# Values in rows of 1 KB beside one block of ones, S2 through GpSimd's queue, three more sums by DMA and a new order: sketched attention followed by a rational mixture layer

## The chip, the cores and the metric

One Trainium2 chip, one of its cores. The metric is the device time of one execution in microseconds (us). Three runs of the kernel before gave 252.32, 252.56 and 252.72, so its median is 252.56 us.

## What is computed

The attention replaces the softmax by a product of two linear sketches of 8 columns each, so keys and queries become 64 features per head. A rational function stands between two matrix products behind it.

```python
def phi(x):                                   # 32 -> 64 features
    a = np.einsum('rd,bhsd->bhsr', S1, x)
    b = np.einsum('rd,bhsd->bhsr', S2, x)
    return np.einsum('bhsi,bhsj->bhsij', a, b).reshape(*x.shape[:-1], 64)
q_p, k_p = phi(q), phi(k)                     # batch 4, heads 4, 1088 tokens
kv = np.einsum('bhsf,bhsd->bhfd', k_p, v)
z = np.sum(k_p, axis=2)
x = einsum(q_p, kv) / (einsum(q_p, z) + 1e-6) # -> [4352, 128]
h = x @ w_in                                  # [4352, 2048]
P = a[0] + a[1]*h + a[2]*h**2 + a[3]*h**3
Q = 1 + |b[0]|*|h| + |b[1]|*h**2
out = (P / (Q + 1e-6)) @ w_out                # [4352, 128]
```

## The kernel before

**Tiles and groups.** The 4352 tokens are cut into chunks of 512. The first chunk is split into two of 256 (called 0 and 0b), and the last, also of 256, holds the 64 tokens of each batch that don't fill a chunk. For each chunk the hidden layer (2048 columns, 16 blocks of 128) is worked in groups. Groups 0 to 3 are the blocks of chunk 0 (2, 2, 4 and 8 of them), group 4 is the whole of chunk 0b, groups 5 to 18 are two for each of the seven full chunks, and groups 19 to 22 (8, 4, 3 and 1 blocks) belong to the last chunk. A full group is a tile of 128x4096.

**One group.** TensorE multiplies `h` into PSUM (L793, a tile of 128x1024 at a time). ScalarE copies it to bf16 as `hb` (L799). For the groups in CASTS one of these four copies is made by VectorE. VectorE takes |h| into `u` (L808, step abs) and h squared into `lin` (L816, step sq). The sum `u += lin` (step +Q) gives the denominator, from which ScalarE makes 1/Q with a logarithm (L830, step Ln, which writes `L`) and an exponential (L833, step Exp, back into `u`). VectorE builds the numerator in `y` (L820 odd, L826 oddt, L823 even), then `y += lin` (step +P), then y times u (step n5, L826), and TensorE multiplies by w_out (L846). The letters in PLANS say who does what in a group: with Q or P that sum is done by a DMA which adds in flight (L882, issued by GpSimd), without it by VectorE (L878). With z the constant term of the numerator is given to TensorE as a second product with a scaled w_out (`w_out_0`), and VectorE's step even is left out. A new letter, s, which is already in the code, lets ScalarE make the square.

**Attention.** Keys of a batch are transposed (L451), copied (L455), sketched (L460), copied (`ab`, L467) and multiplied into features (`k_p`, L478), then summed against the values (L495, kv). The values stand in `v_aug`, head by head, 32 columns and a column of ones beside each, so a matmul takes 66 columns for two heads and the column of ones gives z. For batch 0 the values land in a spare tile first and GpSimd copies them (L437); for the other batches four DMAs write them in pieces of 128 bytes. Queries go a like way (L601, L611, L649, L657), and x comes from L669. Chunks 0 and 0b come early: they don't wait for the matrix W_abc, but take numerator and denominator from one product (L677), add 1e-6 (L688), invert (L692) and divide (L698).

**What sets the order.** Every step is put into a plan with its predecessors. The table ORDER, 773 step numbers, says in what order the steps are issued, and each engine works through its own steps in that order. A step that waits holds back everything behind it on its engine. DMAs of one issuer are likewise started in order. Buffers are counted in BUFS: three each of hb, u, lin and y. SyncE's queue (SP) holds the loads and stores, ScalarE's queue S1 and S2, and GpSimd's queue (POOL) the small loads and the sums by DMA. The steps called hot (L1002) are products of zeros that keep TensorE occupied.

Of the kernel before, what the change touches and what calls it, by code (L numbers as in the profile page):

```python
# [123 lines left out]
def kernel(  # L124
# [74 lines left out]
    v_aug = [big.tile([128, H, J, D + 1], FP, name=f"v_aug{i}") for i in range(2)]  # L199

    def load_main(eng, name, src, b, part=None):
        src = src[b, :, 0:MAIN, :].rearrange("h (p j) d -> p h j d", j=J)
        if name == "v_sb" and b > 0:
            for h in range(H):
                QUEUE[eng].dma_start(out=v_aug[b % 2][:, h, :, 0:D], in_=src[:, h])
            return
# [214 lines left out]
    def scale_w(dst, scale, half):  # L421
        hs = slice(half * NF // 2, (half + 1) * NF // 2)
        if dst is w_out_b:
            return lambda: nc.vector.tensor_scalar(out=dst[:, hs, :], in0=w_out_f[:, hs, :], scalar1=scale, scalar2=None, op0=AX.mult)
# [613 lines left out]
```

## Time and profile before

| | before |
|---|---|
| time, median of 3 runs | 252.56 us (252.32 to 252.72) |
| profiled execution, its own time | 252.38 us |
| span of that execution | 250.7 us |
| granted TensorE clock | 1.00 |
| DMA traffic | 38.51 MB, of it 27.27 MB by GpSimd's queue |
| packets under 512 bytes | 17968 of 31807 |

The profile shows one execution. The span runs from the first to the last instruction; 1.68 us of the execution's own time lie around it. "Busy" is the time in which an engine has at least one instruction under way. Since an instruction is often begun before its predecessor has left the pipe, durations of neighbours overlap, and what an instruction really takes from its engine is the distance between two starts. In a timeline row the first number is the start, the second the duration, and the bracket at the end tells how long the engine stood idle before and what ended that.

### The profile page before, as it was taken

How to read it: one execution, taken by the hardware profiler on the slowest of the kernel's cores; microseconds unless marked ns; L12 is line 12 of the kernel's file. 1: busy time of each engine (PE TensorE's matmuls, PEld its weight loads, DVE VectorE, ACT ScalarE, POOL GpSimd, SP SyncE). 2: the span in 40 equal slices, each digit the busy share in tenths (PEclk: the TensorE clock that was granted, in tenths of full speed). 3: DMA queues.
4: the chain of work that ended last, by engine and by line, in shares of the span. 5: the costliest groups of instructions: out<-in, count | busy, mean ns of one | idle time of the engine just before them, and what ended most of it. 6: DMA issues, size and time to landing. Idle time of an engine off the chain costs nothing.

```text
span 250.7 us, 3050 instructions
## 1 busy us (share of the span) xinstructions
PE 239.3 (95%) x1124; PEld 142.6 (57%) x1135; DVE 229.0 (91%) x243; ACT 221.9 (89%) x201; POOL 49.9 (20%) x68
## 2 busy tenths in 40 slices
PE   8989999999999999999999999999999999999873
PEld 4878888655559655665554544444435444664541
DVE  0647999799999999999999999999999999999991
ACT  3435594799999999999999999999999999999992
POOL 5728003010301113001051101132111111130100
PEclk9999999999999999999999999999999999999999
DMA  6997581998548649980849999598999999699622
GB/s 159 290 280 148 135 150 29 153 221 186 92 76 152 120 86 180 188 156 15 155 84 192 203 190 171 103 181 157 188 181 186 184 168 185 114 223 188 126 86 64
DMA packets 31807, 38.51 MB, mean 154 GB/s; under 512 B 17968, under 2 KB 23600, under 8 KB 31664
## 3 DMA queue, kind: packets, MB, share of 16 engines
q0 software_dynamic: 7152, 27.27, 61.7%
q1 hardware_dynamic: 24208, 10.95, 17.5%
q8 instruction: 9, 0.15, 0.2%
q10 hardware_dynamic: 432, 0.10, 0.2%
q14 instruction: 6, 0.05, 0.1%
HBM read 8.82 MB, written 2.23 MB: 44 GB/s over the span
## 4 chain that ended last, share of the span: by engine, by line
ACT 52%; PE 18%; DVE 12%; issue 10%; DMA 6%; SPq 1%; ACTq 0%
ACT L L830 17%; ACT u L833 16%; ACT hb L799 11%; PE h_ps L793 8%; DVE y L826 4%; DMA u<-lin 4%; PE w_ps L495 3%; DVE y L820 2%; ACT q_pT L663 2%; DMA k_rem<-in_k_dram 2%; ACT o_sb L851 2%; PE w_ps L657 1%; PE w_ps L460 1%; PE w_ps L1002 1%; ACT xT L717 1%
## 5 line engine op out<-in xcount | busy, mean ns | idle before, releaser
L793 PE MATMUL h_ps<-xT,w_in_sb 128*128 128x512 f32 (+1 forms) x320 | 125.6, 532 | 0.7 <-ACT hb L799 0.6
L793 PEld LDWEIGHTS h_ps<-xT,w_in_sb 128*128 128x128 f32 x320 | 58.2, 190 | 43.0 <-issue 34.1
L799 ACT CAST hb<-h_ps 128x1024 bf16<-128x1024 f32 (+2 forms) x65 | 70.4, 1124 | 6.5 <-PE h_ps L793 6.4
L830 ACT ACTIVATE L<-u,one_ap,kappa 128x4096 f32<-128x4096 bf16 (+5 forms) x23 | 70.5, 3066 | 0.0
L833 ACT ACTIVATE u<-L 128x4096 bf16<-128x4096 f32 (+5 forms) x23 | 66.2, 2879 | 0.1
L882 POOL DMA_DIRECT2D u<-lin x16 | 22.2, 1391 | 129.8 <-ACT u L833 31.2
L816 DVE TENSOR_TENSOR lin<-hb 128x4096 bf16<-128x4096 bf16 (+5 forms) x23 | 39.7, 1727 | 2.5 <-ACT hb L799 2.3
L826 DVE TENSOR_TENSOR y<-y,u 128x4096 bf16<-128x4096 bf16 (+5 forms) x23 | 39.7, 1727 | 0.6 <-ACT u L833 0.3
L826 DVE TENSOR_TENSOR y<-y,hb 128x4096 bf16<-128x4096 bf16 (+5 forms) x23 | 39.7, 1726 | 0.0
L846 PE MATMUL out_ps<-y,w_out_b 128*128 128x512 bf16 (+1 forms) x139 | 30.3, 354 | 1.7 <-DVE y L826 1.5
L820 DVE TENSOR_SCALAR y<-lin,a_t 128x4096 bf16<-128x4096 bf16 (+5 forms) x23 | 24.4, 1059 | 0.0
L846 PEld LDWEIGHTS <-w_out_b 128*128 128x128 bf16 x144 | 14.0, 98 | 16.8 <-issue 5.7
L882 POOL DMA_DIRECT2D y<-lin x11 | 14.2, 1287 | 44.7 <-DVE lin L823 20.8
L808 DVE TENSOR_SCALAR u<-hb 128x4096 int16<-128x4096 int16 (+5 forms) x23 | 21.7, 945 | 0.0
L878 DVE TENSOR_TENSOR y<-y,lin 128x4096 bf16<-128x4096 bf16 (+5 forms) x12 | 15.7, 1306 | 0.1
L495 PE MATMUL w_ps<-v_aug,k_p 128*128 128x66 f32 x128 | 15.7, 272 | 0.0
L495 PEld LDWEIGHTS w_ps<-v_aug,k_p 128*128 128x128 f32 x128 | 15.0, 192 | 1.0 <-issue 0.8
L823 DVE TENSOR_SCALAR lin<-lin,a_t 128x4096 bf16<-128x4096 bf16 (+5 forms) x16 | 14.0, 877 | 1.6 <-DMA u<-lin 1.6
L663 ACT COPY q_pT<-w_ps 128x512 f32<-128x512 f32 (+1 forms) x20 | 12.4, 631 | 3.3 <-PE w_ps L657 3.3
L846 PE MATMUL out_ps<-u,w_out 128*128 128x512 bf16 x55 | 13.0, 379 | 0.0
L478 DVE TENSOR_TENSOR k_p<-ab 128x1024 f32<-128x1024 f32 x8 | 9.8, 1219 | 2.6 <-ACT ab L467 2.6
L1002 PE MATMUL w_ps<-const-float32-0.0 128*128 128x512 bf16 x45 | 11.8, 380 | 0.3
(110 smaller groups left out, 224.1 us busy)
## 6 DMA issues: line engine op xcount, KB each, us to landing
u<-lin POOLq DMA_DIRECT2D x15, 1024.0 KB, 8.7
y<-lin POOLq DMA_DIRECT2D x10, 1024.0 KB, 9.7
out_dram<-oT SPq DMA_DIRECT2D x7, 256.0 KB, 2.6
kq<-in_k_dram SPq DMA_DIRECT2D x3, 512.0 KB, 6.4
v_aug<-in_v_dram SPq DMA_DIRECT2D x12, 128.0 KB, 4.8
kq<-in_q_dram SPq DMA_DIRECT2D x3, 512.0 KB, 4.8
w_in_sb<-in_moe_w_in_dram SPq DMA_DIRECT2D x1, 1024.0 KB, 6.9
kq<-in_k_dram SPq DMA_DIRECT2D x2, 256.0 KB, 3.1
```

Of the source, the lines that this page charges most:

```text
L495: nc.tensor.matmul(T["kv", b][:, hp * 66:(hp + 1) * 66], lhsT=lhs(hp), rhs=rhs(hp), start=(first and hp == 0), stop=final, skip_group_chec ...
L663: nc.scalar.copy(out=T["q_pT", n][:, hp, :W], in_=T["qpTp", n, hp][:, :W])
L793: nc.tensor.matmul(T["h", g, s][:, i * W:(i + 1) * W], lhsT=w_in_sb[:, fi * 128:(fi + 1) * 128], rhs=T["xT", n][:, :W], start=True, stop=True)
L799: copy(out=T["t", g][:, s * W:(s + nsub) * W], in_=T["h", g, s][:, :nsub * W])
L808: nc.vector.tensor_scalar(out=u().bitcast(mybir.dt.int16), in0=ht().bitcast(mybir.dt.int16), scalar1=0x7FFF, scalar2=None, op0=AX.bitwise_and)
L816: nc.vector.tensor_mul(out=sq(), in0=ht(), in1=ht())
L820: nc.vector.tensor_scalar(out=y(), in0=sq(), scalar1=a_t[:, 3:4], scalar2=a_t[:, 1:2], op0=AX.mult, op1=AX.add)
L826: return lambda: nc.vector.tensor_mul(out=out(), in0=in0(), in1=in1())
L830: nc.scalar.activation(out=T["L", g][:, :gw], in_=u(), func=ACT.Ln, bias=one_ap, scale=kappa[:, 2:3])
L833: nc.scalar.activation(out=u(), in_=T["L", g][:, :gw], func=ACT.Exp, scale=-1.0)
L846: nc.tensor.matmul(T["o", n][:, :W], lhsT=w[:, fi, :], rhs=T[src, g][:, i * W:(i + 1) * W], start=(start and i == 0), stop=(stop and i == ...
L882: nc.gpsimd.dma_start(out=dst(), in_=src(), accum_op=AX.add, max_dma_last_dim=GW)
```

## The change

The values stand in `v_aug` as [128, 5, 8, 32]: blocks 1 and 3 hold heads 0 and 1, blocks 0 and 4 heads 2 and 3, and block 2 is all ones and shared by the two pairs. The DMA now writes rows of 1 KB, two DMAs for a batch, and for batch 0 straight into place, so that GpSimd's two copies go. A matmul takes 96 columns for a pair. The values of the leftover tokens are laid out in a like way.

S1 stays on ScalarE's queue, S2 goes to GpSimd's as its first instruction. The identity has a step of its own, and the transposes wait for that alone. `ab` has two buffers instead of one. In chunks 0 and 0b the 1e-6 is put in by a small product with the identity (`den_eps`) before numerator and denominator are added, so VectorE's addition L688 goes. The scaled w_out is made by ScalarE instead of VectorE. The bias of the logarithm is a number in the instruction instead of a tile. XWARM falls from two products of zeros to none.

Groups 8, 11 and 14 get their sum +P by DMA. Group 12 loses z, and group 4 gets s. Groups 11, 13 and 15 give one more copy of h to VectorE. The groups of chunk 0 and those of the last chunk each share one buffer of every kind (PACKED), in place of one buffer per group. ORDER is new throughout; of it the first row is shown.

```diff
-    0, 4, 50, 54, 2, 6, 51, 5, 8, 10, 1, 3, 52, 12, 69, 7, 9, 14, 74, 70, 55, 16, 11, 71, 53, 75, 67, 18, 13, 96,
+    0, 4, 5, 56, 2, 7, 9, 51, 6, 11, 1, 52, 53, 3, 69, 13, 8, 54, 10, 15, 74, 70, 57, 17, 12, 71, 58, 75, 55, 59,
...
-    PLANS = {**{g: "QP" for g in range(4, 20)}, **{g:"Q" for g in (5,8,11)},**{g:"Qz" for g in (14,17)},**{g:"QPz" for g in (12,13,15,16,18)}}
-    CASTS = {18:(6,),16:(6,),14:(6,),12:(6,),17:(6,)}
-    XWARM = (2, 0)
+    PLANS = {**{g: "QP" for g in range(4, 20)}, 5:"Q",17:"Qz",**{g:"QPz" for g in (13,15,16,18)},4:"sQP",14:"QPz"}
+    CASTS = {18:(6,),16:(6,),14:(6,),12:(6,),17:(6,),13:(6,),15:(6,),11:(6,)}
+    PACKED = (0, 9)
+    XWARM = (0, 0)
...
-                kq=3, v_aug=2, kT=2, ab=1, k_p=2, qT=1, abc=1, q_p=1, q_pT=2, den=1,
+                kq=3, v_aug=2, kT=2, ab=2, k_p=2, qT=1, abc=1, q_p=1, q_pT=2, den=1,
...
-    v_aug = [big.tile([128, H, J, D + 1], FP, name=f"v_aug{i}") for i in range(2)]
+    PAIRS = (slice(1, 4, 2), slice(0, 5, 4))
+    WITH_ONES = (slice(1, 4), slice(0, 5, 2))
+    v_aug = [big.tile([128, 2 * NP + 1, J, D], FP, name=f"v_aug{i}") for i in range(2)]
...
         if name == "v_sb":
-            if part == 0:
-                T[name, b] = tile_of(att, "q_p", [128, JC * H, R * R], FP).rearrange("p (h a) (c d) -> p h (a c) d", h=H, d=D)
-            hs = slice(2 * part, 2 * part + 2)
-            QUEUE[eng].dma_start(out=T[name, b][:, hs], in_=src[:, hs])
+            for hp in range(NP) if part is None else (part,):
+                QUEUE[eng].dma_start(out=v_aug[b % 2][:, PAIRS[hp]], in_=src[:, 2 * hp:2 * hp + 2])
             return
...
-    last_of["ACT"] = plan.add("ACT", 1300, lambda: load_small("ACT"), rank=-99, name="load")
+    last_of["ACT"] = plan.add("ACT", 650, lambda: load_small("ACT", 0), rank=-99, name="load")
+    i = plan.add("POOL", 1500, lambda: load_small("POOL", 1), rank=-99.9, name="load S2")
...
-            return lambda: nc.vector.tensor_scalar(out=dst[:, hs, :], in0=w_out_f[:, hs, :], scalar1=scale, scalar2=None, op0=AX.mult)
+            return lambda: nc.scalar.activation(out=dst[:, hs, :], in_=w_out_f[:, hs, :], func=ACT.Copy, scale=scale)
...
-        for hps in pairs:
-            kb.append(plan.add("DVE", 200 if b else 270, lambda hps=hps: kv_blocks(hps), after=[sums[-1], c_ms] + kb[-1:],
+        for hps, done in zip(pairs, sums):
+            kb.append(plan.add("DVE", 200 if b else 270, lambda hps=hps: kv_blocks(hps), after=[done, c_ms] + kb[-1:],
...
+        def den_eps(t):
+            T["nd", n, t] = tile_of(aps, "w_ps", [128, CW], FP)
+            nc.tensor.matmul(nd_parts(t)[0][:, :, 2 * D:], lhsT=ident,
+                             rhs=den_t[n % BUFS["den"]][:, 0:8, R].rearrange("p (g h) -> p g h", h=2), start=True, stop=False,
+                             skip_group_check=True)
...
-            nc.scalar.activation(out=T["L", g][:, :gw], in_=u(), func=ACT.Ln, bias=one_ap, scale=kappa[:, 2:3])
+            nc.scalar.activation(out=T["L", g][:, :gw], in_=u(), func=ACT.Ln, bias=1.0 + 1e-6, scale=kappa[:, 2:3])
```

Three places of the new order matter below. The first is TensorE at the start, where the keys of batch 0 are sketched and summed against the values (S is the sketch, kT the transposed keys, k_p their features). Before:

```order
L460 MATMUL w_ps<-S_105,kT 128x64 x4
L601 MATMUL w_ps<-ident,kq 128x128 x2
L451 MATMUL w_ps<-ident,k_rem 128x128
L460 MATMUL w_ps<-S_105,kT 128x64 x4
L611 MATMUL w_ps<-S_105,qT 128x64 x2
L460 MATMUL w_ps<-S_105,kT 128x64
L495 MATMUL w_ps<-v_aug_90,k_p 128x66 x4
L601 MATMUL w_ps<-ident,kq 128x128 x2
```

And now:

```order
L454 MATMUL w_ps<-S_104,kT 128x64 x8
L595 MATMUL w_ps<-ident,kq 128x128 x2
L445 MATMUL w_ps<-ident,k_rem 128x128
L605 MATMUL w_ps<-S_104,qT 128x64 x2
L454 MATMUL w_ps<-S_104,kT 128x64
L489 MATMUL w_ps<-v_aug_90,k_p 128x96 x8
L489 MATMUL w_ps<-v_rem_aug,k_p_rem_227 128x96
```

The second half of the keys is sketched ahead of the transposes of the leftover keys, no longer behind them, and the first pair of heads is summed to its end in one go.

The second place is ScalarE at its first copies of h. Before:

```order
L605 COPY qT<-w_ps 128x512
L713 COPY xT<-w_ps 128x256
L663 COPY q_pT<-w_ps 128x256 x2
L799 CAST hb<-h_ps 128x512 x2
L455 COPY kT<-w_ps 128x512
L713 COPY xT<-w_ps 128x256
L799 CAST hb<-h_ps 128x1024
```

And now:

```order
L599 COPY qT<-w_ps 128x512
L426 ACTIVATE w_out_b<-L,a_c 128x1024
L615 COPY abc<-w_ps 128x4x2x16
L615 COPY abc<-w_ps 128x4x4x24
L828 CAST hb<-h_ps 128x1024
L657 COPY q_pT<-w_ps 128x256
L828 CAST hb<-h_ps 128x1024
L426 ACTIVATE w_out_b<-L,a_c 128x1024
```

The two halves of the scaled w_out stand among the first copies of h, and chunk 0 begins with its group of 8 blocks instead of its groups of 2.

The third place is ScalarE behind the copies of chunk 0b. Now:

```order
L828 CAST hb<-h_ps 128x1024
L712 COPY xT<-w_ps 128x512
L828 CAST hb<-h_ps 128x1024
L843 ACTIVATE lin<-hb 128x4096
L862 ACTIVATE u<-L 128x512
L599 COPY qT<-w_ps 128x512
L859 ACTIVATE L<-u,kappa 128x1024
L828 CAST hb<-h_ps 128x1024
```

The square of group 4 (L843) stands between chunk 0b's last copy of h and the first copy of the next chunk's.

More of the change, by code (lines that the diff above doesn't have):

```diff
@@ L273 @@
     ld["k", 0, 1] = load("SP", lambda e: load_main(e, "k_sb", k, 0, 1), 256, rank=-98)
-    last_of["ACT"] = plan.add("ACT", 1300, lambda: load_small("ACT"), rank=-99, name="load")
-    ld["s"] = plan.add("ACT", 1, lambda: None, after=[last_of["ACT"]], rank=-99, lag=3400, name="load")
+    last_of["ACT"] = plan.add("ACT", 650, lambda: load_small("ACT", 0), rank=-99, name="load")
+    i = plan.add("POOL", 1500, lambda: load_small("POOL", 1), rank=-99.9, name="load S2")
+    ld["s"] = plan.add("ACT", 1, lambda: None, after=[last_of["ACT"], i], rank=-99, lag=2700, name="land S")
     landed.extend([ld["k", 0]] * 2)
     ld["q", 0] = load("SP", lambda e: load_main(e, "q_sb", q, 0, 0), 128, rank=-97.5, take=["kq"])
-    ld["v", 0] = load("SP", lambda e: load_main(e, "v_sb", v, 0, 0), 256, rank=-97, take=["q_p"])
+    ld["v", 0] = load("SP", lambda e: load_main(e, "v_sb", v, 0, 0), 256, rank=-97, take=["v_aug"])
     ld["kr", 0] = load("SP", lambda e: load_rem(e, k_rem, k, 0), 200, 2, rank=-98)
@@ L287 @@
     ld["k", 1] = load("SP", second["k"], 512, 1, rank=-91, take=["kq"])
-    ld["v", 1] = load("SP", second["v"], 1024, H, rank=-90, take=["v_aug"])
+    ld["v", 1] = load("SP", second["v"], 512, NP, rank=-90, take=["v_aug"])
     ld["q", 1] = load("SP", second["q"], 512, 1, rank=-89, take=["kq"])
@@ L355, in first_warm @@
         warm(ZEROS)
-    c_mask = plan.add("POOL", 1350, pool_mask, rank=-99.5)
-    c_pool = plan.add("POOL", 1950, pool_consts, after=[c_mask], rank=-99)
-    i = plan.add("POOL", 2200, lambda: load_ab("POOL"), after=[c_pool], rank=-98.9, name="load ab")
+    c_mask = plan.add("POOL", 640, pool_mask, rank=-99.5, name="masks")
+    c_id = plan.add("POOL", 600, pool_ident, after=[c_mask], rank=-99.2, name="ident")
+    c_pool = plan.add("POOL", 1500, pool_consts, after=[c_id], rank=-99, name="consts")
+    i = plan.add("POOL", 1350, lambda: load_ab("POOL"), after=[c_pool], rank=-98.9, name="load ab")
     ld["ab"] = plan.add("POOL", 1, lambda: None, after=[i], rank=-98.9, lag=3000, name="land ab")
@@ L418 @@
     c_ms = plan.add("DVE", 200, scale_mask, after=[c_b, c_pool], rank=-97, name="scale mask")
-    c_a = plan.add("DVE", 1500, scale_a, after=[c_b, ld["ab"]], rank=-5, name="scale a")
+    c_a = plan.add("DVE", 1100, scale_a, after=[c_b, ld["ab"]], rank=-5, name="scale a")
     def scale_w(dst, scale, half):
@@ L423, in scale_w @@
         if dst is w_out_b:
-            return lambda: nc.vector.tensor_scalar(out=dst[:, hs, :], in0=w_out_f[:, hs, :], scalar1=scale, scalar2=None, op0=AX.mult)
+            return lambda: nc.scalar.activation(out=dst[:, hs, :], in_=w_out_f[:, hs, :], func=ACT.Copy, scale=scale)
         return lambda: nc.gpsimd.tensor_scalar(out=dst[:, hs, :], in0=w_out_f[:, hs, :], scalar1=scale, scalar2=None, op0=AX.mult)
-    c_w = [plan.add("DVE", 680, scale_w(w_out_b, a2_c[:, 3:4], half), after=[ld["wo"], c_a], rank=-0.25, name=f"w1 {half}") for half in range(2)]
-    c_w0 = [plan.add("POOL", 1400, scale_w(w_out_0, a_sb[:, 0:1], half), after=[ld["wo"], ld["ab"]], rank=-0.2, name=f"w0 {half}") for half in range(2)]
+    c_w = [plan.add("ACT", 930, scale_w(w_out_b, a2_c[:, 3:4], half), after=[ld["wo"], c_a], rank=-0.25, name=f"w1 {half}") for half in range(2)]
+    c_w0 = [plan.add("POOL", 2850, scale_w(w_out_0, a_sb[:, 0:1], half), after=[ld["wo"], ld["ab"]], rank=-0.2, name=f"w0 {half}") for half in range(2)]
     plan.add("DVE", 1, lambda: None, after=c_w + c_w0, rank=-0.1, give=["L"])
@@ L432, in add_keys @@
         T["va", b] = v_aug[b % 2]
-        if b == 0:
-            va = []
-            for hp in range(NP):
-                hs = slice(2 * hp, 2 * hp + 2)
-                va.append(plan.add("POOL", 620, lambda hs=hs: nc.gpsimd.tensor_copy(out=v_aug[0][:, hs, :, 0:D], in_=T["v_sb", b][:, hs]),
-                                   after=[ld["v", b], ld["v", b, 1] if hp else None, c_pool] + va, rank=rank - 1,
-                                   take=[] if hp else ["v_aug"], give=["q_p"] if hp == NP - 1 else [], name=f"va {hp}"))
-        else:
-            va = [ld["v", b]] * NCH
+        va = [ld["v", 0], ld["v", 0, 1]] if b == 0 else [ld["v", b]] * NCH
         if b % 2 == 0:
@@ L756, in add_queries @@
         s = plan.add("PE", 110 * nt, transposes,
-                     after=load_steps + [c_pool] + [T.get(("q tr", n - 1)) if give or early else None], rank=rank, take=["w_ps"],
+                     after=load_steps + [c_id] + [T.get(("q tr", n - 1)) if give or early else None], rank=rank, take=["w_ps"],
                      give=give, name=f"q tr {lab(n)}")
@@ L787, in add_group, with allocate, new, take @@
         first = fis[0] == 0
+        packed = n in PACKED
+        KINDS = dict(t=("hb", "ACT", "DVE", BF), u=("u", "DVE", "DVE", BF), sq=("lin", "DVE", "DVE", BF), y=("y", "DVE", "PE", BF),
+                     L=("L", "ACT", "ACT", FP))
+        def allocate(kind):
+            T[kind, "of", n] = tile_of(moe, KINDS[kind][0], [128, GW], KINDS[kind][3])
+        if packed and first:
+            for kind, (tag, eng, _, _) in KINDS.items():
+                T[kind, "got", n] = plan.add(eng, 1, lambda kind=kind: allocate(kind), after=[G["x_step"]], rank=g - 1.46, take=[tag], name=f"get {tag} {n}")
+                T[kind, "used", n] = []
+        def new(kind):
+            if packed:
+                T[kind, g] = T[kind, "of", n][:, fis[0] * W:(fis[-1] + 1) * W]
+            else:
+                T[kind, g] = tile_of(moe, KINDS[kind][0], [128, GW], KINDS[kind][3])
+        def take(kind):
+            return [] if packed else [KINDS[kind][0]]
+        def got(kind):
+            return [T[kind, "got", n]] if packed else []
+        def used(step, *kinds):
+            if packed:
+                for kind in kinds:
+                    T[kind, "used", n].append(step)
+            return step
+        def give(*kinds):
+            return [] if packed else [KINDS[kind][0] for kind in kinds]
         def h_mm(s, nsub):
@@ L811, in square @@
         def square():
-            T["sq", g] = tile_of(moe, "lin", [128, GW], BF)
+            new("sq")
             if "s" in how:
@@ L902, in add_group @@
                           after=[e, rt] + c_w0[:1 + (fis[-1] >= NF // 2)], rank=g + 0.45, take=["out_ps"] if first else [], name=f"pr {g}")
-        p = add_up("+P", y, sq, [p, v, dq0], g - 0.3, give=["lin"])
-        p = plan.add("DVE", tt, mul(y, y, u), after=[p, e], rank=g + 0.55, give=[] if z else ["u"], name=f"n5 {g}")
+            used(rt, "u")
+        p = used(add_up("+P", y, sq, [p, v, dq0], g - 0.3, give=give("sq")), "sq")
+        p = used(plan.add("DVE", tt, mul(y, y, u), after=[p, e], rank=g + 0.55, give=[] if z else give("u"), name=f"n5 {g}"), "u")
         o = plan.add("PE", len(fis) * pw, lambda: project("y", w_out_b, first and not z, final), after=[p, rt] + c_w[:1 + (fis[-1] >= NF // 2)], rank=g + 0.56,
-                     take=["out_ps"] if first and not z else [], give=["u", "y"] if z else ["y"], name=f"py {g}")
+                     take=["out_ps"] if first and not z else [], give=give("u", "y") if z else give("y"), name=f"py {g}")
+        used(o, "y")
+        if packed and final:
+            for kind, (tag, _, eng, _) in KINDS.items():
+                plan.add(eng, 1, lambda: None, after=T[kind, "used", n], rank=g + 0.6, give=[tag], name=f"give {tag} {n}")
         if final and by_token:
```

93 lines of the change are left out of this document (42 added, 51 removed), and 68 rows, old and new, of the table ORDER.

## The prediction

> **What bounds the kernel now.** I read the page first, then busy time by stages, then ScalarE's timeline.
>
> ```profile
> span 250.7 us, 3050 instructions
> PE 239.3 (95%) x1124; PEld 142.6 (57%) x1135; DVE 229.0 (91%) x243; ACT 221.9 (89%) x201; POOL 49.9 (20%) x68
> ...
> ACT 52%; PE 18%; DVE 12%; issue 10%; DMA 6%; SPq 1%; ACTq 0%
> ```
>
> Three engines are nearly full, and half of the chain that ended last is ScalarE (ACT). The stages tell more (columns: stage, its length, then busy time and count for PE, PEld, VectorE = DVE, ACT, POOL, then clock, share of the DMA engines, GB/s):
>
> ```profile
> 0.00:20.00 20.00, 18.12 (x116) 14.65 (x118) 7.07 (x21) 7.33 (x18) 10.58 (x40) 1.00 0.86 232
> 20.00:57.40 37.40, 36.47 (x215) 28.97 (x215) 35.30 (x73) 25.99 (x37) 7.25 (x4) 1.00 0.80 144
> 57.40:100.00 42.60, 42.55 (x203) 25.47 (x203) 42.50 (x34) 42.49 (x40) 7.53 (x6) 1.00 0.67 125
> 100.00:150.00 50.00, 49.84 (x210) 27.51 (x211) 49.84 (x37) 50.00 (x41) 7.36 (x6) 1.00 0.81 147
> 150.00:200.00 50.00, 49.27 (x172) 22.78 (x174) 49.55 (x36) 50.00 (x36) 10.52 (x8) 1.00 0.93 169
> 200.00:235.00 35.00, 34.30 (x157) 18.76 (x159) 34.66 (x26) 35.00 (x23) 6.65 (x6) 1.00 0.92 172
> 235.00:245.20 10.20, 6.95 (x54) 3.81 (x53) 9.80 (x20) 10.10 (x12) 0.00 (x0) 1.00 0.35 92
> ...
> 94.00:111.50 17.50, 17.45 (x76) 9.80 (x76) 17.34 (x15) 17.50 (x15) 2.39 (x2) 1.00 1.02 180
> ```
>
> From 57.4 to 245.2 us ACT never rests. DVE rests 1.45 us there, beside it. So the end is ACT's load plus ACT's idle time ahead of 57.4: 12.7 us up to 20, and 11.4 from 20 to 57.4. DVE has nearly the same balance, so a gain needs both. What an instruction costs is the distance between starts:
>
> ```profile
> 112.74 3.92 ACT L830 ACTIVATE L<-u,one_ap,kappa 128x4096 f32<-128x4096 bf16 x1
> 116.45 2.03 ACT L799 CAST hb<-h_ps 128x1024 bf16<-128x1024 f32 x2
> 118.24 0.72 ACT L717 COPY xT<-w_ps 128x512 f32<-128x512 f32 x1
> 118.72 3.76 ACT L833 ACTIVATE u<-L 128x4096 bf16<-128x4096 f32 x1
> 122.24 0.72 ACT L663 COPY q_pT<-w_ps 128x512 f32<-128x512 f32 x1
> ```
>
> A Ln takes 3.71 us, an Exp 3.52, a copy of h 0.90.
>
> **The work that changes hands.**
>
> ```profile
> L816 DVE TENSOR_TENSOR lin<-hb 128x4096 bf16<-128x4096 bf16 x15 | 34.3, 2284 | 0.1
> ...
> L495 PE MATMUL w_ps<-v_aug,k_p 128*128 128x66 f32 x128 | 15.7, 272 | 0.0
> ...
> L1002 PE MATMUL w_ps<-const-float32-0.0 128*128 128x512 bf16 x45 | 11.8, 380 | 0.3
> L878 DVE TENSOR_TENSOR y<-y,lin 128x4096 bf16<-128x4096 bf16 x5 | 11.4, 2287 | 0.1
> ...
> L823 DVE TENSOR_SCALAR lin<-lin,a_t 128x4096 bf16<-128x4096 bf16 x8 | 10.2, 1278 | 1.6 <-DMA u<-lin 1.6
> ...
> L611 PE MATMUL w_ps<-W_abc,qT 128*128 128x96 f32 x56 | 7.4, 275 | 0.1
> ...
> L799 DVE CAST hb<-h_ps 128x1024 bf16<-128x1024 f32 x5 | 6.1, 1220 | 0.2 <-PE h_ps L793 0.2
> ...
> L424 DVE TENSOR_SCALAR w_out_b<-L,a_c 128x1024 bf16<-128x1024 f32 x2 | 1.5, 738 | 0.0
> ...
> L688 DVE TENSOR_SCALAR den<-w_ps 128x8 f32<-128x8 f32 x2 | 0.3, 172 | 1.0 <-PE w_ps L677 1.0
> ```
>
> Each duration holds some 0.08 us that overlap the next instruction.
> - DVE: three sums +P go (3 x 2.20 = -6.6), and the square of group 4 (-2.2), two halves of w_out (-1.3), two additions of 1e-6 (-0.3). Three copies of h come (3 x 1.14 = +3.4), and group 12's step even, which z had spared (+1.2). Sum: **-5.8 us**.
> - ACT: the square of 4096 elements comes, priced as the Exp (+3.5), and two halves of w_out, priced as copies of h (+1.9). Three copies of h go (-2.7). The Ln reads two columns of constants where the Exp reads none, and costs 0.19 more; one of the two goes. That saves between nothing and 0.19 for each of 23 Ln (0 to 4.4 us). I take half, since the two columns are alike: -2.1. Sum: **+0.6 us**. The Trainium skill (ScalarE: Activation LUTs, What ACT_TABLE_LOAD costs) puts each such operand at about 93 ns; by it the saving would be 2.1 us too, and the two operands' 0.19 us here agree with twice that.
> - TensorE: 96 columns where 66 were. The two rows show 272 ns for 66 columns and 275 for 96, so 144 instructions cost 0 to 0.4 us; I take 0. The four instructions that put in the 1e-6 cost at most 4 x 0.28, ahead of products that wait for kv anyway: 0. Group 12's eight products for z go, under 3 us; TensorE isn't the last anywhere behind 57.4 us (11.8 us of products of zeros stand where it would wait), so I count nothing.
> - POOL's two copies of values go. They fed products that waited for k_p anyway: 0. PACKED adds no instruction; it could only make a later group wait for a buffer, and the new order puts chunk 0's last products (n5) ahead of group 6: 0.
>
> So the load of ACT hardly falls. What matters is whether its new work fits into its idle time, and whether it becomes full sooner.
>
> **The opening.** TensorE, DVE, POOL and ACT at the start, and the first full chunk's products:
>
> ```profile
> 3.29 0.73 POOL L239 DMA_DIRECT2D b_sb<-in_moe_b_dram  x1
> ...
> 5.05 0.24 DVE L364 STREAM_TRANSPOSE sT<-SR 128x64 f32<-128x64 f32 x1 [5.05 <-DMA SR<-in_S_dram]
> ...
> 5.93 1.31 PE L460 MATMUL w_ps<-S,kT 128*128 128x64 f32 x8
> ...
> 7.82 0.30 PE L451 MATMUL w_ps<-ident,k_rem 128*128 128x128 f32 x1 [0.35 <-DMA k_rem<-in_k_dram]
> ...
> 14.88 0.22 DVE L550 TENSOR_TENSOR kv_bd<-w_ps,mask2s 128x64 f32<-128x64 f32 x1 [1.59 <-PE w_ps L495]
> ```
> ```profile
> 18.39 5.67 POOL L425 TENSOR_SCALAR w_out<-L,a_sb 128x1024 bf16<-128x1024 f32 x2 [4.96 <-DMA L<-in_moe_w_out_dram]
> ```
> ```profile
> 18.73 0.86 PE h_ps L793 x4
> ```
> ```profile
> 45.59 1.96 PE L793 MATMUL h_ps<-xT,w_in_sb 128*128 128x512 f32 x4
> ```
>
> Now the second sketch of keys stands ahead of the transposes that waited for k_rem until 7.82, so it runs right behind the first, about a us sooner (`ab` has a second buffer for it); the sums of the first pair end near 11.3 and those of the second near 13.7, where DVE had waited until 14.88. Between the two stand the 13 small operations of scale_a, some 2 us, which end near 14.7; the rest of the way (product, reciprocal, divide, transpose, copy) is as long as before without the addition and the products of zeros. First product h: about 17.2 instead of 18.73, **1.5 us sooner**. From there to the first full chunk TensorE has 26.9 us of work, of which about 1.1 (four transposes, the sketch of the leftover keys, two products with w_out) now stands behind: 45.59 becomes about 43, **2.6 us sooner**. S2 costs POOL one issue of 0.73 us ahead of the identity, or 2 us by POOL's longest issue below; the transposes that need the identity wait for keys until shortly before 5.93, so that is covered. S was there at 5.05 and its first user began at 5.93, behind a copy, so S2 may land up to half a us later for nothing; beyond that the whole opening is later by as much. ACT's first half of w_out waits for the load that landed at 18.39, about a us, in time that was idle before; the copies of h behind it start near 20, as before.
>
> ACT's new 5.4 us fall before 45 us, where ACT had over 20 us of idle time: the w_out halves among the first copies of h, the square in the hole before the first full chunk. They cost nothing there; uncovered they would cost 5.4. So ACT's idle time falls by 5.4 + 2.6 = 8.0, its load grows by 0.6, and its end moves by **-7.4**.
>
> DVE's moves by -5.8 and by a wait that goes:
>
> ```profile
> 40.50 1.97 POOL L882 DMA_DIRECT2D u<-lin  x1 [16.44 <-ACT ab L470]
> ```
> ```profile
> 45.64 0.37 SPq L225 DMA_DIRECT2D kq<-in_k_dram  x1
> 46.06 6.33 SPq L205 DMA_DIRECT2D v_aug<-in_v_dram  x4
> ```
> ```profile
> 50.44 1.29 DVE L823 TENSOR_SCALAR lin<-lin,a_t 128x4096 bf16<-128x4096 bf16 x1 [1.62 <-DMA u<-lin]
> ```
>
> Group 4's sum took 10 us, since batch 3's keys and values (in pieces of 128 bytes) were loaded into it. These loads now wait for transposes near 50 us, and the sum is over by then; the values also come in 1 KB. DVE: -5.8 - 1.6 = **-7.4**. Both engines come out alike.
>
> **The DMA queue takes some back.** Three sums stand in a row:
>
> ```profile
> 92.35 1.19 POOL L882 DMA_DIRECT2D y<-lin  x1 [8.55 <-DVE lin L823]
> 97.89 1.19 POOL L882 DMA_DIRECT2D u<-lin  x1 [4.36 <-ACT u L833]
> 99.20 1.20 POOL L882 DMA_DIRECT2D y<-lin  x1
> ```
>
> They kept the DMA engines busy from 94 to 111.5 (the last stage row, share 1.02): 5.8 us each. Three more are 17.4 us. From 57.4 to 235 the share left 14.1 + 9.5 + 3.5 + 2.8 = 29.9 us free, so they fit, but not where they come: groups 13 to 16 now have two sums each in a row, 11.6 us, while ACT needs 3 copies, Ln, Exp and a store's two copies, 2.7 + 3.6 + 3.5 + 1.0 = 10.8. The queue falls behind by 0.8 in each of four groups, 3.2 us, and ACT's Ln waits for its sum. Before, groups 14 and 17 had one sum each and the queue caught up. I take **+3.0** (bounds 0 and 17.4). The Trainium skill (DMA: Bandwidth & Descriptors, Anatomy of one DMA) has 2.0 us plus bytes at 436 GB/s, so 2.4 us for each sum that follows another; by it there would be no lag and the sum would be 3.0 lower. The 180 GB/s of these three speak against it for sums.
>
> **Sum.** Span 250.7 - 7.4 + 3.0 = 246.3; with the 1.68 us around it (252.38 - 250.7) **248.0**. The profiled execution is 0.18 under the median of 252.56, which is nothing beside the rest. A measurement of this kernel can tell about 0.2% from no change.
>
> **Rivals.**
> - *The queue keeps up.* Sums +P are needed late (three buffers of y), so the lag may fall on nothing. Then 252.4 - 7.4 = 245.0. For it: DMA was busy at 0.93 from 150 to 200 and ACT never waited. Against it: 0.93 leaves 3.5 us for a sum of 5.8. Chance 0.20, in it the faster sums by the skill's rule 0.02.
> - *The opening gives little.* If ACT becomes full no sooner, or its new work isn't covered, ACT's idle time falls by some 3 instead of 8: 252.4 + 0.6 - 3 + 1.5 = 251.5. For it: a long chain in four engines, in which one late copy moves all. Chance 0.13.
> - *Slower: the queue becomes the bound.* If the sums wait on one another from group 6 on, where each group now has two, the 29.9 us of free DMA time can't be used, since a sum can't start before its operands. From 7.4 of the 17.4 us on the path the change is a loss; with two thirds, 11.6, it gives 252.4 - 7.4 + 11.6 = 256.6. For it: every group from 6 to 16 has two sums, 11.6 us against steps of 10.8 to 13. Chance 0.12.
> - Forecast, 246.0 to 250.0: 0.55.
>
> The forecast and the first rival are faster, and about two thirds of the second: 0.84 faster, 0.04 within 0.2%, 0.12 slower. The range: 244.5 takes in the queue that keeps up; 252.0 takes in the opening that gives little and the lower end of a lag of 7. The Ln's bounds (2.1 either way) lie inside.
>
> **What would show it.** First product h near 17.2 us and the first of 128x512 near 43. ACT without a wait from about 45 us, busy for about 222.5 in all; DVE busy for about 223. No wait of DVE for group 4's sum. Ln 3.62 us between starts. From 150 to 230 a DMA share near 1.0, and waits of ACT's Ln for "DMA u<-lin" of about 3 us in total. The prediction is wrong if these waits are over 7 us or absent, if ACT still rests 20 us in its first 57, or if matmuls of 96 columns stand further apart than those of 66.

## The result and the profile after

| | before | changed |
|---|---|---|
| time, median of 4 runs each | 252.44 us (252.29 to 252.72) | 248.49 us (248.25 to 248.79) |
| ratio, with its 95% interval | | 0.9843 (0.9826 to 0.986) |
| span of the profiled execution | 250.7 us | 246.3 us |
| GpSimd's queue | 27.27 MB | 30.43 MB |
| packets under 512 bytes | 17968 of 31807 | 5504 of 21662 |

The kernel became 1.6% faster. Time and span came out close to the prediction (248.0 and 246.3), but not all of the terms did. First the page of the changed kernel, then its busy times by stages (columns as before: stage, length, PE, PEld, VectorE, ScalarE, POOL, clock, DMA share, GB/s):

```profile
span 246.3 us, 3019 instructions
PE 238.5 (97%) x1119; PEld 140.3 (57%) x1129; DVE 222.9 (90%) x239; ACT 222.8 (90%) x201; POOL 55.0 (22%) x69
```
```profile
0.00:20.00 20.00, 17.96 (x117) 14.11 (x118) 8.30 (x34) 7.26 (x16) 11.99 (x38) 1.00 0.89 261
20.00:57.40 37.40, 37.40 (x207) 28.55 (x206) 32.12 (x56) 32.86 (x42) 5.71 (x4) 1.00 0.46 112
57.40:100.00 42.60, 42.55 (x209) 25.79 (x209) 42.08 (x32) 42.09 (x37) 7.04 (x6) 1.00 0.83 154
100.00:150.00 50.00, 49.71 (x211) 27.29 (x212) 49.41 (x40) 48.82 (x41) 12.31 (x9) 1.00 1.00 178
150.00:200.00 50.00, 49.56 (x170) 22.31 (x172) 49.86 (x37) 49.69 (x39) 11.46 (x9) 1.00 1.03 191
200.00:230.00 30.00, 29.03 (x140) 16.26 (x141) 30.00 (x25) 29.66 (x18) 5.64 (x5) 1.00 1.02 188
```

ScalarE's rests up to 57.4 us were 24.1 us and are 12.7 + 4.5 = 17.3. Behind 57.4 us, where it had rested 0.2 us, it now rests 2.4. The waits of ScalarE from there on show for whom (columns: who waited for whom, us in total, times, longest):

```profile
ACT hb L828 <- PE h_ps L822: 1.6, 4, 0.7
ACT L L859 <- DMA u<-lin: 0.3, 1, 0.3
ACT oT L944 <- PE out_ps L870: 0.2, 1, 0.2
```

So it waits for TensorE's products, and hardly for the sums. VectorE's own list from 45 us on has no wait for a DMA left:

```profile
DVE y L855 <- ACT u L862: 0.8, 3, 0.4
DVE y L849 <- PE out_ps L875: 0.3, 1, 0.3
DVE hb L828 <- PE h_ps L822: 0.2, 1, 0.2
```

TensorE's timeline has the first product h and the first one of 512 columns (18.73 and 45.59 us before):

```profile
17.85 1.97 PE L822 MATMUL h_ps<-xT,w_in_sb 128*128 128x256 f32 x8
...
44.02 1.88 PE L822 MATMUL h_ps<-xT,w_in_sb 128*128 128x512 f32 x4
```

Between 20 and 57.4 us it now never rests: 37.40 us busy of 37.40.

### The profile page after: what moved, and what is told of

Read it like the earlier page. It is cut to its first block, busy times and chain, and to the rows that moved or that the text cites. A ratio compares the mean times of both kernels' runs of the same rounds, so it can differ in the third digit from the quotient of the medians.

```text
span 246.3 us, 3019 instructions
## 1 busy us (share of the span) xinstructions
PE 238.5 (97%) x1119; PEld 140.3 (57%) x1129; DVE 222.9 (90%) x239; ACT 222.8 (90%) x201; POOL 55.0 (22%) x69
## 2 busy tenths in 40 slices
DMA packets 21662, 41.65 MB, mean 169 GB/s; under 512 B 5504, under 2 KB 12688, under 8 KB 21520
## 3 DMA queue, kind: packets, MB, share of 16 engines
q0 software_dynamic: 8000, 30.43, 69.3%
## 5 line engine op out<-in xcount | busy, mean ns | idle before, releaser
L822 PE MATMUL h_ps<-xT,w_in_sb 128*128 128x512 f32 (+1 forms) x320 | 127.1, 534 | 0.7 <-ACT hb L828 0.7
L828 ACT CAST hb<-h_ps 128x1024 bf16<-128x1024 f32 (+3 forms) x62 | 61.4, 1009 | 4.3 <-PE h_ps L822 4.0
L859 ACT ACTIVATE L<-u,kappa 128x4096 f32<-128x4096 bf16 (+5 forms) x23 | 65.0, 2830 | 0.3 <-DMA u<-lin 0.3
L862 ACT ACTIVATE u<-L 128x4096 bf16<-128x4096 f32 (+5 forms) x23 | 63.0, 2749 | 0.1
L845 DVE TENSOR_TENSOR lin<-hb 128x4096 bf16<-128x4096 bf16 (+5 forms) x22 | 37.3, 1702 | 2.2 <-ACT hb L828 2.1
L911 POOL DMA_DIRECT2D y<-lin x14 | 17.5, 1251 | 69.4 <-DVE lin L852 19.6
L489 PE MATMUL w_ps<-v_aug,k_p 128*128 128x96 f32 x128 | 15.6, 276 | 0.0
L657 ACT COPY q_pT<-w_ps 128x512 f32<-128x512 f32 (+1 forms) x20 | 10.5, 558 | 3.8 <-PE w_ps L651 3.8
L643 DVE TENSOR_TENSOR q_p<-abc 128x1024 f32<-128x1024 f32 (+1 forms) x10 | 10.6, 1062 | 1.1 <-ACT abc L615 1.0
L875 PE MATMUL out_ps<-u,w_out 128*128 128x512 bf16 x46 | 11.2, 379 | 0.3 <-ACT u L862 0.2
```

The lines of the kernel that those rows point to most:

```text
L489: nc.tensor.matmul(T["kv", b][:, hp * 96:(hp + 1) * 96], lhsT=lhs(hp), rhs=rhs(hp), start=(first and hp == 0), stop=final, skip_group_chec ...
L822: nc.tensor.matmul(T["h", g, s][:, i * W:(i + 1) * W], lhsT=w_in_sb[:, fi * 128:(fi + 1) * 128], rhs=T["xT", n][:, :W], start=True, stop=True)
L828: copy(out=T["t", g][:, s * W:(s + nsub) * W], in_=T["h", g, s][:, :nsub * W])
L845: nc.vector.tensor_mul(out=sq(), in0=ht(), in1=ht())
L859: nc.scalar.activation(out=T["L", g][:, :gw], in_=u(), func=ACT.Ln, bias=1.0 + 1e-6, scale=kappa[:, 2:3])
L862: nc.scalar.activation(out=u(), in_=T["L", g][:, :gw], func=ACT.Exp, scale=-1.0)
```

## The experiments

All start from the changed kernel. "Ratio" is against runs of the kernel before made beside the run, with its 95% interval; the changed kernel has 0.9843. The kernel before took 252.44 us beside the changed kernel and 252.1 to 252.5 beside the experiments, so differences of 0.3 us between rows say little. "Span" is that of the profiled execution, to be held against 246.3. In the diffs `...` stands for code left out; with an edit go the lines that make or fill its tiles, and in e2, e3, e9 and e11 the table ORDER moves or renumbers the steps concerned. Where an edit adds lines, the line numbers behind it shift by a few.

| run | edit | time, us | ratio | span, us |
|---|---|---|---|---|
| e1 | bias of the Ln from a tile | 249.40 | 0.9875 (0.9856 to 0.9895) | 247.6 |
| e2 | three sums back on VectorE | 254.78 | 1.0090 (1.0072 to 1.0107) | 252.7 |
| e3 | w_out and square back on VectorE | 249.69 | 0.9898 (0.9870 to 0.9925) | 247.5 |
| e4 | three copies of h back on ScalarE | 251.03 | 0.9943 (0.9925 to 0.9960) | 249.0 |
| e5 | 2.2 us of zeros on TensorE, 30 us | 250.69 | 0.9942 (0.9927 to 0.9958) | 248.6 |
| e6 | the same at 104 us | 250.27 | 0.9924 (0.9906 to 0.9942) | 248.1 |
| e7 | values in pieces of 128 bytes | 248.25 | 0.9845 (0.9826 to 0.9863) | 246.6 |
| e8 | four half sums more in the queue | 257.84 | 1.0223 (1.0207 to 1.0240) | 255.7 |
| e9 | z for group 12 again | 250.13 | 0.9922 (0.9906 to 0.9938) | 248.6 |
| e10 | 2.2 us of zeros at 165 us | 250.27 | 0.9926 (0.9911 to 0.9941) | 248.5 |
| e11 | one sum more by DMA (group 5) | 248.35 | 0.9855 (0.9839 to 0.9870) | 246.3 |
| e12 | S2 back on ScalarE's queue | 248.39 | 0.9854 (0.9837 to 0.9871) | 246.2 |

Much is read below from one series: the starts of the logarithms of 4096 elements in ScalarE's timeline, one for each group. The first row has them for the changed kernel, the others how much later they start.

| logarithm of group | 4 | 8 | 9 | 12 | 13 | 14 | 16 | 18 |
|---|---|---|---|---|---|---|---|---|
| changed kernel, us | 55.86 | 112.39 | 123.43 | 160.83 | 173.53 | 184.24 | 206.12 | 225.18 |
| e1 | +0.23 | +0.42 | +0.46 | +0.52 | +0.52 | +0.52 | +0.46 | +0.79 |
| e2 | +0.09 | +0.10 | +0.10 | +4.04 | +4.03 | +4.04 | +5.53 | +6.42 |
| e3 | +0.97 | +1.33 | +1.33 | +1.34 | +1.34 | +1.34 | +1.20 | +1.21 |
| e4 | -0.02 | -0.02 | +2.58 | +2.06 | +2.06 | +2.60 | +2.47 | +2.67 |
| e5 | +2.26 | +2.26 | +2.26 | +2.49 | +2.49 | +2.49 | +2.00 | +2.29 |
| e6 | -0.09 | +1.82 | +1.82 | +1.82 | +1.81 | +1.82 | +1.85 | +1.83 |
| e8 | -0.04 | -0.04 | -0.04 | -0.04 | -0.05 | +0.45 | +7.08 | +9.45 |
| e9 | +0.43 | +0.44 | +0.44 | +0.45 | +0.44 | +2.17 | +1.68 | +2.32 |
| e10 | +0.46 | +0.47 | +0.46 | +0.47 | +2.41 | +2.41 | +1.92 | +2.25 |

In e9 and e10 the 0.44 stand there long before the edit; the opening of these two profiled executions was that much later.

### e1: the bias in a tile again

```diff
-  ... func=ACT.Ln, bias=1.0 + 1e-6, scale=kappa[:, 2:3])
+  ... func=ACT.Ln, bias=one_ap, scale=kappa[:, 2:3])
```

> The changed kernel with the bias of the 23 logarithms in a tile of ones again, nothing else. Theory A (ScalarE and VectorE are both full from 45 us on, so what is added to ScalarE there comes out at the end): a logarithm of 4096 elements stands 3.70 us from the next start instead of 3.61, ScalarE is busy 2.1 us longer (224.9), and the time is 249.5 to 250.6, the lower end if the 2.1 us that ScalarE still rests behind 57 us take up some of it. Rival B (the DMA queue, whose share is 1.00 to 1.03 from 100 to 230 us, sets the pace there, so a little work on ScalarE is hidden): 248.3 to 248.8.

Measured: 249.40. ScalarE's timeline, the same logarithm and what follows it, in the changed kernel and in e1:

```profile
112.39 3.71 ACT L859 ACTIVATE L<-u,kappa 128x4096 f32<-128x4096 bf16 x1
116.00 1.00 ACT L828 CAST hb<-h_ps 128x1024 bf16<-128x1024 f32 x1
```
```profile
112.81 3.81 ACT L861 ACTIVATE L<-u,one_ap,kappa 128x4096 f32<-128x4096 bf16 x1
116.51 1.01 ACT L830 CAST hb<-h_ps 128x1024 bf16<-128x1024 f32 x1
```

The distance of starts is 3.61 without the tile and 3.70 with it, as expected. ScalarE has 1.9 us more work (224.7), but only 0.9 us come out, just under theory A's range (1.3 us in the span; there the other 0.6 went into ScalarE's rests, which shrank). So ScalarE alone doesn't set the pace.

### e2: the three sums on VectorE again

```diff
-  ... 5:"Q",17:"Qz",**{g:"QPz" for g in (13,15,16,18)},4:"sQP",14:"QPz"}
+  ... 5:"Q",8:"Q",11:"Q",17:"Qz",**{g:"QPz" for g in (13,15,16,18)},4:"sQP",14:"Qz"}
```

> The changed kernel with the sums +P of groups 8, 11 and 14 on VectorE again, each at the place where the DMA was issued. VectorE gets 3 x 2.2 = 6.6 us of work, the queue loses 3 x 5.8 = 17.4 us. Theory A (VectorE rests under 1 us from 57 to 230 us and the queue costs nothing worth naming): 254.0 to 255.2. Rival B (the queue takes back the 3.0 us that the prediction gave it): those 3 us return, 251 to 252. DMA share from 100 to 150 us falls from 1.00 to about 0.85 in both.

Measured: 254.78, theory A. Its busy times by stages:

```profile
100.00:150.00 50.00, 48.31 (x202) 25.87 (x203) 49.68 (x38) 46.93 (x41) 9.04 (x7) 1.00 0.84 150
150.00:200.00 50.00, 46.68 (x160) 20.67 (x161) 49.86 (x39) 47.72 (x35) 8.01 (x6) 1.00 0.71 132
```

VectorE is busy 229.2 us, 6.3 more, and the time grows by 6.3. The DMA share falls from 1.00 and 1.03 to 0.84 and 0.71, and nothing of that comes back. With the 0.3 us that ScalarE waits for sums in the changed kernel, this says that the queue takes no time worth naming there.

### e3: the opening's work on VectorE again

```diff
-  return lambda: nc.scalar.activation(out=dst[:, hs, :], in_=w_out_f[:, hs, :], func=ACT.Copy, scale=scale)
+  return lambda: nc.vector.tensor_scalar(out=dst[:, hs, :], in0=w_out_f[:, hs, :], scalar1=scale, scalar2=None, op0=AX.mult)
...
-  ... 4:"sQP",14:"QPz"}
+  ... 14:"QPz"}
```

> The changed kernel with the two halves of the scaled w_out and the square of group 4 on VectorE again: ScalarE loses 5.9 us of work before 45 us, VectorE gets 3.5. Theory A (TensorE, which never rests from 18 to 57 us, sets the pace of the opening, so ScalarE's 5.9 us stood in rests and come back as rests; the square falls on VectorE at 41 to 45 us where it doesn't rest, the two halves near 24 us where it does): ScalarE's last Exp at most 1 us sooner by itself, VectorE 2.2 later, so 249.5 to 251. Rival B (ScalarE's work in the opening is on the path): 244 to 246. Rival C (all 3.5 us of VectorE count): 252.

Measured: 249.69, theory A. ScalarE loses 5 us of work (217.8) and gains nothing by it: that work had been covered. The 1.2 us of loss begin at one place, in VectorE's and TensorE's timeline (the bracket: how long it stood idle, and for whom):

```profile
42.25 2.29 DVE L845 TENSOR_TENSOR lin<-hb 128x4096 bf16<-128x4096 bf16 x1
...
46.64 0.38 PE L557 MATMUL w_ps<-z_bd,S2x 128*128 128x32 f32 x2 [0.81 <-DVE z_bd L552]
```

The square stands ahead of VectorE's small steps for batch 1, and TensorE waits for one of them, z_bd. The first logarithm is 0.97 later, the next ones 1.3.

### e4: three copies of h on ScalarE again

```diff
-  CASTS = {18:(6,),16:(6,),14:(6,),12:(6,),17:(6,),13:(6,),15:(6,),11:(6,)}
+  CASTS = {18:(6,),16:(6,),14:(6,),12:(6,),17:(6,)}
```

> The changed kernel with the fourth copy of h of groups 11, 13 and 15 on ScalarE again: ScalarE +2.7 us, VectorE -3.4, at about 120, 145 and 180 us. Theory A (both full, ScalarE's load comes out at the end): 250.5 to 251.3. Rival B (the queue or VectorE alone sets the pace): 247 to 248.5.

Measured: 251.03, theory A's number, but not by the load. ScalarE's timeline:

```profile
125.10 1.01 ACT L828 CAST hb<-h_ps 128x1024 bf16<-128x1024 f32 x1 [1.58 <-PE h_ps L822]
126.01 3.71 ACT L859 ACTIVATE L<-u,kappa 128x4096 f32<-128x4096 bf16 x1
```

Group 11's copy stands ahead of group 9's logarithm and waits 1.58 us for its product: the logarithm is 2.6 later at once (123.43 in the changed kernel), and behind it the shift stays between 2.0 and 2.8: the other two copies add next to nothing. This run prices one place of the order, not three copies.

### e5 and e6: products of zeros on TensorE

```diff
   T["h", g, s] = tile_of(hps, "h_ps", [128, 1024], FP)
+  for _ in range(10 if g == 4 and s == 0 else 0):
+      nc.tensor.matmul(T["h", g, s][:, :CW], lhsT=zero.broadcast_to([128, 128]), rhs=zero.broadcast_to([128, CW]), start=True, stop=True)
```

In e6 the group is 10.

> The changed kernel with ten products of zeros (128x512 bf16, about 0.22 us each, 2.2 us in all) on TensorE ahead of group 4's first product h, near 31 us. Theory A (TensorE sets the pace of the opening: it never rests from 17.6 to 57.4 us, and ScalarE and VectorE wait for it there): the first 512-column product h starts at 46.2 instead of 44.0, and most of it comes out at the end, 249.8 to 250.7. Rival B (ScalarE is full from 29.3 us on by its own work, so a later TensorE is hidden): 248.3 to 248.9.

> The same ten products of zeros ahead of group 10's first product h, near 95 us. Theory A (behind 57 us TensorE's work is less than ScalarE's and VectorE's, it only looks full because it is spread out): 248.3 to 249.2, a part of it seen as a wait of ScalarE for h_ps there. Rival B (TensorE, busy 97% of the span, sets the pace everywhere): 250.2 to 250.8.

Measured: 250.69 and 250.27. TensorE's timeline of e5, then TensorE's and ScalarE's rows of e6:

```profile
30.37 2.35 PE L821 MATMUL h_ps<-const-float32-0.0 128*128 128x512 bf16 x10
...
46.29 1.88 PE L824 MATMUL h_ps<-xT,w_in_sb 128*128 128x512 f32 x4
```
```profile
104.27 2.35 PE L821 MATMUL h_ps<-const-float32-0.0 128*128 128x512 bf16 x10
```
```profile
108.37 1.01 ACT L830 CAST hb<-h_ps 128x1024 bf16<-128x1024 f32 x1 [1.41 <-PE h_ps L824]
```

In e5 the logarithms are 2.0 to 2.5 later, from the first to the last. I had expected e6 to be hidden (theory A), and that was wrong: 1.8 of the 2.2 us come out, and from group 8 on the shift stays what it is. So TensorE has next to no room behind 57 us either.

### e7: pieces of 128 bytes

```diff
-  v_aug = [big.tile([128, 2 * NP + 1, J, D], ...) for i in range(2)]
+  v_aug = [big.tile([128, J, 2 * NP + 1, D] if i else [128, 2 * NP + 1, J, D], ...) for i in range(2)]
...
```

> The changed kernel with the values of batches 1 and 3 in pieces of 128 bytes again (their tile as 8x5x32 instead of 5x8x32, four DMAs for a batch; the matmuls keep 96 columns). Theory A (the pieces fall into group 4's sum, which runs from about 47 to 54 us and lands 1.6 us ahead of the logarithm that needs it, as the prediction put it for the kernel before): the first logarithm of 4096 elements starts 1 to 2 us later than 55.86, and the time is 249.3 to 250.5. Rival B (the loads now stand where the queue has room; their layout is worth nothing): 248.3 to 248.8. DMA share from 45 to 57.4 us rises from 0.75 to 0.9 or more in both.

Measured: 248.25, theory B; theory A was mine and fell. DMA share from 45 to 57.4 us rose only from 0.75 to 0.82. But the run doesn't put the pieces into group 4's sum, as its expectation had it. SyncE's queue starts the values of batch 3 at 52.50 us, and from 46.5 to 52.4 us only GpSimd's queue moves bytes, nearly the whole sum (queue, packets, MB, share of the 16 DMA engines):

```profile
52.50 4.08 SPq L212 DMA_DIRECT2D v_aug<-in_v_dram  x4
```
```profile
q0 software_dynamic: 246, 1.01, 96.3%
```

In the kernel before, from 48 to 51 us, the sum (q0) and the loads (q1) ran side by side:

```profile
q0 software_dynamic: 48, 0.13, 52.8%
q1 hardware_dynamic: 424, 0.43, 40.7%
```

So for these two batches, where their loads now stand, rows of 1 KB are worth nothing that can be measured. What pieces of 128 bytes cost beside a sum, e7 doesn't show.

### e8: more work for the full queue

```diff
   nc.gpsimd.dma_start(out=dst(), in_=src(), accum_op=AX.add, max_dma_last_dim=GW)
+  if name == "+P" and g in (13, 14, 15, 16):
+      nc.gpsimd.dma_start(out=v_aug[0][:, 0:4]..., in_=w_out_0..., accum_op=AX.add, max_dma_last_dim=GW)
```

> The changed kernel with an additional DMA of half a sum's size (w_out_0 added onto a tile of values that nobody reads any more) behind each of the sums +P of groups 13, 14, 15 and 16, 2.9 us each, 11.6 us in all, where the DMA share is 1.03. Theory A (the queue runs level with ScalarE there: its lag is hidden by a us or two of slack, no more): logarithms 14 to 18 wait for their sums, 6 to 10 us in all, and the time is 254.5 to 258.5. Rival B (the queue has room behind the full share, since e2's 17.4 us less gave nothing back): 248.4 to 249.5.

Measured: 257.84, theory A. ScalarE's waits from 57.4 us on:

```profile
ACT L L859 <- DMA u<-lin: 9.5, 4, 3.9
ACT hb L828 <- PE h_ps L822: 1.6, 4, 0.7
```

Of 11.6 us (by the estimate of 2.9 for half a sum) 9.4 come out. So the queue runs level with the engines from 160 us on, with about 2 us to spare by that estimate: it costs next to nothing yet, but takes nothing more.

### e9 and e10: TensorE late in the kernel

```diff
-  ... **{g:"QPz" for g in (13,15,16,18)} ...
+  ... **{g:"QPz" for g in (12,13,15,16,18)} ...
```

e10 is e5's edit for group 16.

> The changed kernel with z for group 12 again: TensorE makes eight more products of 512 bf16 columns (8 x 0.216 = 1.7 us), just ahead of group 12's products with w_out_b near 175 us, VectorE loses the step even (1.2 us) near 158. Theory A (TensorE sets the pace up to there, as the ten products of zeros near 95 us showed by adding 1.8 of their 2.2 us): 249.3 to 250.2. Rival B (the prediction's: TensorE isn't the last anywhere behind 57 us, so only VectorE's 1.2 us less count): 247.3 to 248.5.

> The ten products of zeros (2.2 us) ahead of group 16's first product h, near 170 us. TensorE rests 0.4 us from 150 to 200 and 1.0 from 200 to 230. Theory A (TensorE still sets the pace, with about a us of slack): 249.2 to 250.2. Rival B (the queue and VectorE set the pace there): 248.3 to 249.0. Rival C (no slack at all): 250.3 to 250.8.

Measured: 250.13 and 250.27. TensorE's timeline of e9 at the added products:

```profile
175.02 1.89 PE L875 MATMUL out_ps<-u,w_out 128*128 128x512 bf16 x8
176.75 1.89 PE L875 MATMUL out_ps<-y,w_out_b 128*128 128x512 bf16 x8
178.47 1.88 PE L822 MATMUL h_ps<-xT,w_in_sb 128*128 128x512 f32 x4
```

They take 1.73 us, and the logarithm of group 14 is later by as much (2.17 - 0.44), though VectorE has 1.2 us less to do. In e10 1.9 of 2.2 us come out, 1.8 of them at the last logarithm. TensorE has no room there either; e10's 250.27 is a trifle above theory A's range.

### e11: one sum more where the queue stands idle

```diff
-  ... 5:"Q",17:"Qz" ...
+  ... 17:"Qz" ...
```

> The changed kernel with one more sum by DMA, +P of group 5, which falls where the queue stands idle (behind group 6's sum, 78 to 84 us); group 5's product y times u comes two steps later. VectorE loses 2.2 us near 66 us. Theory A (up to 150 us TensorE sets the pace, so relief for VectorE there is worth nothing): 248.1 to 248.8, VectorE rests about 2 us more from 57 to 100 us. Rival B (VectorE sets the pace, as three sums more on it cost 6.3 us): 246.2 to 247.2.

Measured: 248.35, theory A. The stage and VectorE's longest wait in it:

```profile
57.40:100.00 42.60, 42.60 (x210) 25.73 (x209) 40.02 (x31) 42.09 (x37) 8.11 (x7) 1.00 0.96 178
```
```profile
DVE u L838 <- ACT hb L829: 2.3, 1, 2.3
```

VectorE's 2 us became a wait of 2.3 us. Relief for this one engine is worth nothing here, near 66 us, while 6.3 us more on the same engine in later groups (e2) cost 6.3.

### e12: S2 on ScalarE's queue

```diff
-  i = plan.add("POOL", 1500, lambda: load_small("POOL", 1), rank=-99.9, name="load S2")
+  i = plan.add("ACT", 1500, lambda: load_small("ACT", 1), rank=-99.9, name="load S2")
```

> The changed kernel with S2 on ScalarE's queue behind S1 again, as in the kernel before. Theory A (S2's place is worth nothing: S is there before the first keys are copied either way): 248.2 to 248.8. Rival B (S2 lands later behind S1, and every tenth of a us of the opening comes out at the end, as the products of zeros ahead of group 4 showed): 248.9 to 249.5.

Measured: 248.39, theory A. No experiment was measurably faster than the changed kernel: e7, e11 and e12 have its time within 0.1%.

## Why the prediction came out right, and where it was wrong

**The opening** was right in kind and a little too large. The first product h came at 17.85 us, not 17.2, the first of 512 columns at 44.02, not 43. ScalarE's rests fell by 6.8 us, not 8.0. That ScalarE's new work is covered was right (e3). What governs the opening is TensorE, as e5 shows: 2.2 us more of TensorE at 30 us are 2.2 us more of the kernel. How much of the gain the new order brings there is read from the traces alone, since no run puts the old order back.

**The loads** were right: ScalarE 222.8 us (said 222.5), VectorE 222.9 (said 223). A half of w_out took 1.05 us, not 0.90. The saving per logarithm was right (0.09 us), but as e1 shows not its price: of 2.1 us counted on ScalarE, 0.9 are on the path.

**The queue's +3.0 was wrong.** The lag didn't reach ScalarE: its logarithms waited 0.3 us in all, where about 3 were forecast and none at all was named as a sign of being wrong, and e2 gave nothing back. One part of it can be read from the starts: the logarithms of groups 12 to 16 stand 11.3 us apart ((206.12 - 160.83) / 4), not 10.8, so against 11.6 us for two sums the queue falls behind by 0.3 us in each group instead of 0.8. That the queue would be full, and would soon be the bound, was right (e8). The rival in which the queue keeps up had the mechanism, and still the wrong time.

**The other step that failed** is "TensorE isn't the last anywhere behind 57.4 us (11.8 us of products of zeros stand where it would wait), so I count nothing". The prediction took their sum as room everywhere. Of the 45 in that row, TensorE's timeline of the kernel before has only these seven ahead of 216 us:

```profile
142.64 1.47 PE L1002 MATMUL w_ps<-const-float32-0.0 128*128 128x512 bf16 x5
151.69 0.60 PE L1002 MATMUL w_ps<-const-float32-0.0 128*128 128x512 bf16 x2
```

Over most of the kernel, then, they are no sign of slack, and in the changed kernel TensorE has next to no room there: e6, e9 and e10 brought out 1.8 of 2.2, 1.7 of 1.7 and 1.8 of 2.2 us. So group 12's products for z, counted at nothing, would cost 1.7 us if they came back (e9), and most of what ScalarE waits behind 57 us it waits for TensorE (1.6 of 2.4 us). In the new order even these zeros have gone from the middle; the first ones in TensorE's timeline come at the end:

```profile
219.89 5.41 PE L1036 MATMUL w_ps<-const-float32-0.0 128*128 128x512 bf16 x23
```

The seven that stood in the middle are another 1.5 us or so less on TensorE which the prediction didn't see; what it is worth was not tried.

ScalarE's true sum: rests up to 57.4 us -6.8, load +0.9, rests behind it +2.2, and 0.7 less behind its last Exp, where the last stores land: -4.4, as the span has it. In the prediction: -8.0 + 0.6 + 3.0 = -4.4. The 3.0 that the queue didn't take were made up by an opening 1.2 smaller, a load 0.3 larger and 2.2 of rests, mostly for TensorE, less the 0.7 at the end. The total is right because the errors cancelled, and that was luck.

**Group 4's sum.** The wait went as forecast, and the first reason given holds: the loads of batch 3's values are now issued at 52.27 us, and by 52.4 us the whole sum has been moved (1.05 MB); in the kernel before both ran side by side (rows at e7). Whether the rows of 1 KB have a share in it stays open, since in e7 too the pieces come behind the sum; no run moves the loads alone.

**96 columns, S2, POOL's copies**, all counted at nothing: for S2's place e12 shows it. Of the columns, TensorE's timeline has 32 products of batch 2 in 3.62 us with 66 columns (77.75 to 81.37) and in 3.64 with 96 (74.32 to 77.96). The copies, PACKED, the second buffer of `ab` and the small products for the 1e-6 were not tried alone.

**Why an addition counts and a relief doesn't.** From 57 to 230 us TensorE rests 1.8 us, ScalarE 2.3 and VectorE 1.3, of 172.6 each, and the sums' queue has about 2 us to spare by the estimate from e8. (TensorE's 5.4 us of zeros from 219.89 us on are counted as busy; up to there it rests 1.2 us.) Each engine works through a fixed order. A delay on any of them is handed to the others, and none has rest enough to make it up: e5's shift is 2.26 us at 56 us and 2.29 at 225. A relief on one only lets it wait for the next: e11 for VectorE, e3 for ScalarE's work in the opening, e2 for the queue. By this the change gained since it took work or waiting from all at once, which is argued and not shown, for no run takes work from TensorE alone: 6.1 us off VectorE's work, 6.8 off ScalarE's rests in the opening, and for TensorE a first full chunk 1.6 us sooner and 1.7 us of products.

## What to carry to other kernels

Where several engines are busy over 97% of a stage, as here, don't name one of them the bound: price a change on each engine's own column, and take the least gain and the largest loss. Test TensorE with a few products of zeros at three places, since its busy share alone doesn't tell whether it is full or merely stretched. And look where products of zeros stand in the program before taking them as slack.
